# Pair-by-pair products in a PSUM tile of their own kind, halved first roots, and a newly searched order

## The chip, the cores and the metric

The kernel runs on one core of a Trainium2 chip. The metric is the device time of one launch in microseconds. A core has five instruction streams: TensorE (matmul, with its weight loads shown apart), VectorE, ScalarE, GpSimd, and SyncE, which only issues DMAs here. Matmul results land in PSUM, of which a core has eight banks.

## What is computed

Three blocks in a row, on 4 batches of 448 tokens and 768 features (12 heads of 64): attention with RMS-normalised queries and keys, a spatial gating block (called MoE in the program), and a mixer over tokens and channels.

```python
q_n, k_n = rmsnorm(q, g_q), rmsnorm(k, g_k)
scores = q_n @ k_n.T / sqrt(64)
attn = exp(scores - max) / (sum + 1e-09)
x = attn @ v                                   # heads side by side: (4, 448, 768)

h = relu(x @ w_in); u, v = h[..., :512], h[..., 512:]
v_n = (v - mean(v)) / sqrt(var(v) + 1e-06)
gated = u * (w_spatial @ v_n + b_spatial)
x = gated @ w_out

u = x + w_tok2.T @ relu(w_tok1.T @ x)          # over tokens
out = u + relu(u @ w_ch1) @ w_ch2
```

All inputs are float32. Most products are taken with operands split into a high and a low part and three matmuls (high by high, high by low, low by high: PASSES in the program).

## The kernel before

The heads are worked in pairs, 24 in all, six to a batch. For a pair the kernel squares and sums Q and K, takes the reciprocal roots, rescales, transposes Q and K on TensorE (`transposed`), multiplies scores in four row groups of 112 tokens (`scores`, c from 0 to 3, two heads each), takes the maximum on VectorE and the exponential on ScalarE, transposes the exponentials (`turned`), multiplies them with V (`values`), and leaves the pair's output as a high and a low part in a tile xp. The first eight pairs use plain float32 matmuls (WHOLE), the others the split. `slot(s)` lists the pieces of one step, which work on pairs s - 1 to s + 2.

The very first pair has a path of its own, `first` (line 794): K's squares on ScalarE (`squares`), their sum on VectorE and the roots on VectorE (`root`, through `rsqrt`, line 698), the rescaling of K on VectorE (`scale`), its transposes, and the copy out of PSUM on ScalarE, scaled by gg, the product of the two gains, which `start` (line 1009) computes on VectorE. Q of the first pair isn't rescaled: its roots, worked out on GpSimd, go into the exponential as its scale.

The MoE of a batch (`moe`, line 1218) starts with four groups of 128 tokens (the last of 64, padded by its low parts), each a PSUM tile vps. A group is the sum over the six pairs of the batch, with three matmuls of 512 columns for each pair, 18 in all: `xs[j]`, the xp tile of pair j, by `wv[:, w, j]`, the split weights of that pair's features. `prepare_v` makes wv beside the attention, on ScalarE, VectorE and GpSimd. The helper `run` issues the 18 in three pieces of six.

Nothing runs in the order in which it is written. Every call is kept as an operation in a `Plan`, and `issue` (line 413) puts them in order: `place` (line 272) simulates the engines with estimated costs and takes, of the operations that are ready, the one with the smallest weight; the weights come from rounds forwards and backwards, and are then changed by the numbers in NUDGES, each of which moves the weights of some operations about one place by a drawn amount (`nudged`, line 516). NUDGED bounds where that place may lie. The plan knows that VectorE and GpSimd share a port (`op.port`, line 176) and that a change between half-array and full-array matmuls costs TensorE time.

PSUM's eight banks are given out by `Banks` (line 132) in kinds: sc for scores, tp for transposes, mm for everything else before the mixer, values and vps among them. OWN says how many banks are kept for a kind; here two for sc, two for tp and one for mm, so three are spare. Tiles of a kind are opened in the order in which the program lists them, so a vps listed after a values tile can't be opened before it. BACK says how far back in its kind a tile's predecessor is taken to be in the backward round. Every instruction shows line 464, that of the call in `issue`; tiles tell them apart.

Of the kernel before, what the change touches and what calls it, by code (L numbers as in the profile page):

```python
# [15 lines left out]
AF = mybir.ActivationFunctionType  # L16
ALU = mybir.AluOpType
# [114 lines left out]
class Banks:  # L132
# [3 lines left out]
    OWN = {"sc": 2, "tp": 2, "mm": 1}  # L136
# [16 lines left out]
class Plan:  # L153
# [8 lines left out]
    def add(self, engine, fn, args, kwargs):  # L162
# [6 lines left out]
        if out is None:  # L169
# [7 lines left out]
            len(sbuf) > 1 and free(sbuf[1].shape) > 1  # L177
            or len(ins) == len(sbuf) and fn in ("tensor_scalar", "tensor_copy"))
# [288 lines left out]
BACK = {"sc": 4, "tp": 2, "mm": 2}  # L467
# [4 lines left out]
NUDGED = 4000  # L472
NUDGES = (
# [21 lines left out]
)  # L495
ENGINES = "gpsimd", "scalar", "sync", "tensor", "vector"
IDLE, SPARE, PACE = 1500, 200, 546
SHARED = {"vector": "gpsimd", "gpsimd": "vector"}


# [61 lines left out]
def attention_moe_mixer(  # L562
# [14 lines left out]
    P = 128  # L577
# [1099 lines left out]
```

## Time and profile before

| | us |
|---|---|
| median of 3 runs | 847.92 |
| fastest and slowest of them | 847.16, 848.81 |
| the profiled execution | 847.23 |
| span of its instructions | 845.2 |
| TensorE busy | 833.1 |
| VectorE busy | 674.7 |
| ScalarE busy | 526.7 |
| GpSimd busy | 344.6 |

The span runs from the first to the last instruction; the profiled execution took 2.0 us more than it. Busy times are sums over stages of different character: up to about 120 us the first batch's attention runs with preparation of weights beside it, up to 406 us attention and MoE are mixed, and after that TensorE works on the last MoE and the mixer. The granted TensorE clock is full throughout. In the rows below, a name like vps<-wv,xp gives the tile that is written and the tiles that are read, and x12 the number of instructions that a line merges.

### The profile page before, as it was taken

What the parts mean: (1) busy time and instruction counts of PE and PEld (TensorE: products, weight loads), DVE (VectorE), ACT (ScalarE), POOL (GpSimd) and SP (SyncE); (2) the same over time, 40 slices, a digit from 0 to 9 for tenths busy, and PEclk for the clock granted to TensorE, in tenths of its full rate; (3) what the DMA queues carried; (4) which work ended last, traced back from release to release, by engine and by line L of the source; (5) the groups of instructions that cost most, each with busy time, mean ns of one, the idle gap of its engine ahead of it and who ended that gap; (6) DMA issues with size and microseconds to landing.
All of it is one profiled execution on the core that took longest, in us unless ns stands there. A gap on an engine that the chain in (4) does not pass through costs nothing.

```text
span 845.2 us, 16488 instructions
## 1 busy us (share of the span) xinstructions
PE 833.1 (99%) x5530; PEld 700.4 (83%) x5530; DVE 674.7 (80%) x1340; ACT 526.7 (62%) x1268; POOL 344.6 (41%) x431
## 2 busy tenths in 40 slices
PE   7999999999999999999999999999999999999998
PEld 5454567777678876787799999999999999999998
DVE  6899899886787778787475677988889876998863
ACT  6999899897776878766343565554345654343331
POOL 2457555663445524242152222525331018515460
PEclk9999999999999999999999999999999999999999
DMA  6656676766765866466968787667555635742441
GB/s 170 161 160 185 177 232 184 236 169 170 241 184 144 216 171 196 124 180 194 331 201 247 234 275 252 220 197 221 156 175 175 214 123 161 226 140 84 140 142 66
DMA packets 158532, 157.94 MB, mean 187 GB/s; under 512 B 79216, under 2 KB 141616, under 8 KB 158448
## 3 DMA queue, kind: packets, MB, share of 16 engines
q1 hardware_dynamic: 157984, 156.86, 62.1%
q8 instruction: 44, 0.72, 0.4%
q14 instruction: 40, 0.33, 0.1%
q10 hardware_dynamic: 464, 0.03, 0.0%
HBM read 117.95 MB, written 38.88 MB: 186 GB/s over the span
## 4 chain that ended last, share of the span: by engine, by line
PE 82%; ACT 9%; DMA 3%; DVE 3%; issue 1%; SPq 1%; POOL 0%; ACTq 0%; POOLq 0%; DVEq 0%
PE o_ps L464 18%; PE h2ps L464 18%; PE xps L464 7%; PE ups L464 7%; PE av L464 6%; PE vps L464 5%; PE tp L464 5%; PE sc L464 4%; PE sps L464 4%; ACT e L464 4%; PE h1ps L464 4%; PE u_ps L464 3%; ACT et L464 2%; ACT sq L464 1%; DMA raw<-in_k_dram 1%
## 5 line engine op out<-in xcount | busy, mean ns | idle before, releaser
L464 PE MATMUL h2ps<-op,w 128*128 128x448 f32 x756 | 154.1, 366 | 0.0
L464 PEld LDWEIGHTS o_ps<-w,op 128*128 128x128 f32 x900 | 154.0, 188 | 0.0
L464 PE MATMUL o_ps<-w,op 128*128 128x384 f32 (+1 forms) x900 | 153.9, 332 | 0.0
L464 PEld LDWEIGHTS h2ps<-op,w 128*128 128x128 f32 x756 | 141.6, 188 | 11.2
L464 ACT ACTIVATE e<-sc,nm 112x448 f32<-112x448 f32 x184 | 121.7, 692 | 5.5 <-DVE nm L464 5.3
L464 DVE TENSOR_REDUCE nm<-sc 112x1 f32<-112x448 f32 x192 | 110.2, 615 | 8.0 <-PE sc L464 7.3
L464 ACT ACTIVATE op<-c 128x768 fp32r<-128x768 f32 x49 | 41.5, 847 | 83.7 <-PE o_ps L464 77.3
L464 POOL TENSOR_TENSOR src<-src 128x384 f32<-128x384 f32 x48 | 61.2, 1284 | 73.4 <-DMA src<-c_d 56.1
L464 PEld LDWEIGHTS tp<-ident,e 64*128 64x128 f32 (+2 forms) x1120 | 55.5, 139 | 27.4 <-ACT e L464 9.5
L464 ACT ACTIVATE et<-tp 128x448 f32<-128x448 f32 (+1 forms) x144 | 72.7, 560 | 4.9 <-PE tp L464 4.5
L464 DVE TENSOR_SCALAR word<-word 128x256 f32<-128x256 f32 (+5 forms) x132 | 60.5, 462 | 18.4 <-ACT word L464 17.3
L464 DVE SCALAR_TENSOR_TENSOR word<-raw,word 128x256 uint32<-128x256 uint32 (+2 forms) x132 | 71.2, 541 | 1.8
L464 POOL TENSOR_TENSOR u<-u,o 128x384 f32<-128x384 f32 x28 | 40.5, 1464 | 68.4 <-ACT o L464 38.9
L464 PE MATMUL tp<-ident,e 48*128 48x48 f32 (+2 forms) x1120 | 65.4, 232 | 1.2 <-ACT e L464 0.8
L464 PE MATMUL ups<-xp,wu 128*128 128x448 f32 x288 | 65.9, 368 | 0.0
L464 DVE TENSOR_TENSOR op<-c,op 128x768 fp32r<-128x768 f32 x49 | 54.6, 1115 | 10.3 <-ACT op L464 10.3
L464 PE MATMUL av<-et,v 128*64 128x448 f32 x288 | 61.1, 550 | 1.4 <-ACT e L464 0.9
L464 PEld LDWEIGHTS ups<-xp,wu 128*128 128x128 f32 x288 | 53.7, 188 | 6.4 <-ACT e L464 0.7
L464 DVE TENSOR_TENSOR c<-c,h2ps 128x448 f32<-128x448 f32 x84 | 49.7, 613 | 8.4 <-PE h2ps L464 8.2
L464 PE MATMUL xps<-wo,g 128*128 128x384 f32 x288 | 55.1, 340 | 0.0
L464 PE MATMUL sc<-kt,qt 64*112 64x448 f32 x384 | 52.9, 384 | 0.0
L464 PE MATMUL vps<-wv,xp 128*128 128x512 f32 x216 | 52.8, 397 | 0.0
(146 smaller groups left out, 1595.1 us busy)
## 6 DMA issues: line engine op xcount, KB each, us to landing
src<-c_d SPq DMA_DIRECT2D x132, 192.0 KB
wu<-wu_d SPq DMA_DIRECT2D x16, 768.0 KB
wo<-wo_d SPq DMA_DIRECT2D x16, 768.0 KB
raw<-in_moe_w_ch_dram SPq DMA_DIRECT2D x36, 256.0 KB
raw<-in_moe_w_ch_dram SPq DMA_DIRECT2D x24, 384.0 KB
raw<-in_q_dram SPq DMA_DIRECT2D x48, 112.0 KB
over<-over_d SPq DMA_DIRECT2D x48, 112.0 KB
u<-u_d SPq DMA_DIRECT2D x28, 192.0 KB
```

What stands on the lines that cost most here:

```text
L464: getattr(getattr(self.nc, op.engine), fn)(*args, **kwargs)
```

## The change

The edits, with the two lists of NUDGES cut. 233 numbers take the place of 231.

```diff
-    OWN = {"sc": 2, "tp": 2, "mm": 1}
+    OWN = {"sc": 2, "tp": 2, "mm": 1, "av": 0}
...
         op.port = engine == "gpsimd" and bool(sbuf) or engine == "vector" and (
-            len(sbuf) > 1 and free(sbuf[1].shape) > 1
-            or len(ins) == len(sbuf) and fn in ("tensor_scalar", "tensor_copy"))
+            len(sbuf) > 1 and (fn == "tensor_tensor" or free(sbuf[1].shape) > 1)
+            or len(ins) == len(sbuf) and fn in ("tensor_scalar", "tensor_copy") and free(ins[0].shape) > 1)
...
-BACK = {"sc": 4, "tp": 2, "mm": 2}
+BACK = {"sc": 4, "tp": 2, "mm": 2, "av": 1}
...
-NUDGED = 4000
+NUDGED = 4006
 NUDGES = (
...
-    for i in range(max(0, at - reach), min(len(weight), at + reach)):
+    for i in range(max(0, at - reach), min(NUDGED, at + reach)):
...
                 if on is nc.scalar:
-                    on.activation(sq, raw[:, a], AF.Square)
+                    for h in (slice(0, C), slice(C, n)):
+                        on.activation(sq[:, h], raw[:, a, h], AF.Square)
...
-                nc.vector.reduce_sum(ss[:T], sq, axis=AX.X)
+                for h in (slice(0, C), slice(C, n)):
+                    nc.vector.reduce_sum(ss[:T, h], sq[:, h], axis=AX.X)
...
-            for a in range(2) if i else (1,):
+            if not i:
+                roots = self.r[0][1][:T]
+                for c in range(0, C, 2):
+                    raw = self.raw[0][:, 1, c:c + 2].rearrange("p c r d -> p (c r) d")
+                    nc.vector.tensor_tensor(
+                        raw, raw, roots[:, 2 * c:2 * c + 4].unsqueeze(2).to_broadcast([T, 4, D]), op=ALU.mult)
+                return
+            for a in range(2):
...
-            nc.scalar.activation(t, tpf, AF.Copy, scale=1.0 if a == 0 else self.gg[:, 0:1])
+            if a and not i:
+                n = S // 2
+                nc.scalar.activation(t[:, :n], tpf[:, :n], AF.Copy, scale=self.gg[:, 0:1])
+                nc.vector.tensor_scalar(t[:, n:], tpf[:, n:], self.gg[:, 0:1], None, ALU.mult)
+            else:
+                nc.scalar.activation(t, tpf, AF.Copy, scale=1.0 if a == 0 else self.gg[:, 0:1])
...
-            nc.vector.tensor_tensor(self.gg, g[:, 0:1], g[:, 1:2], op=ALU.mult)
-            nc.vector.tensor_scalar(self.gg, self.gg, float(D) ** -0.5, None, ALU.mult)
+            nc.gpsimd.tensor_tensor(self.gg, g[:, 0:1], g[:, 1:2], op=ALU.mult)
+            nc.gpsimd.tensor_scalar(self.gg, self.gg, float(D) ** -0.5, None, ALU.mult)
...
             self.scores(s, 0)
+            self.scores(s, 1)
             yield
             self.turned(s - 1, 2)
+            self.turned(s - 1, 3)
             yield
-            self.turned(s - 1, 3)
             self.transposed(s + 1, 0)
+            self.transposed(s + 1, 1)
             yield
-            self.scores(s, 1)
-            self.transposed(s + 1, 1)
             self.values(s - 1)
             yield
             self.scores(s, 2)
+            self.scores(s, 3)
             yield
...
-            self.scores(s, 3)
             self.divisors(s)
...
-            ps = mm_tile("vps")
+            ps = psum.tile([P, 512], "av" if b < 1 and t < 1 * P else "mm", "vps")
             vr = mp.tile([P, DU], F32, tag="vr", bufs=2, name="vr")
             if m == P:
-                yield from run(
-                    ps[:, :DU], [(xs[j][:, a, t:t + m], wv[:, w, j]) for j in range(KD) for a, w in PASSES], 6)
+                ops = [(xs[j][:, a, t:t + m], wv[:, w, j]) for j in range(KD) for a, w in PASSES]
+                if b == 0 and t == 0:
+                    for k in range(0, len(ops), 3):
+                        with nc.joined_up():
+                            for i, (lhs, rhs) in enumerate(ops[k:k + 3], k):
+                                nc.tensor.matmul(ps[:, :DU], lhs, rhs, start=not i, stop=i == len(ops) - 1)
+                        yield
+                else:
+                    yield from run(ps[:, :DU], ops, 6)
```

The first token group of the first batch gets a PSUM kind of its own, av, with no bank kept for it; its three matmuls of each pair are joined into one operation. The first pair's squares, sums and rescaling are made in halves, and the copy of its transposed K is shared by ScalarE and VectorE. The two operations of gg go to GpSimd. The pieces of a slot are listed in another order. The plan's rule on the shared port counts other operations. NUDGES is another list, and no longer reaches past operation 4006.

## Rows read from the trace of the kernel before

**Rows 1.** The page: TensorE's busy time, and its busy tenths in 40 slices.

```profile
PE 833.1 (99%) x5530; PEld 700.4 (83%) x5530; DVE 674.7 (80%) x1340; ACT 526.7 (62%) x1268; POOL 344.6 (41%) x431
PE   7999999999999999999999999999999999999998
```

**Rows 2.** Windows of 20 us: busy us of each engine, clock, DMA share, GB/s.

```profile
0.00:20.00 20.00, 14.80 (x91) 11.43 (x91) 11.75 (x31) 12.63 (x32) 5.72 (x23) 1.00 0.68 166
20.00:40.00 20.00, 19.07 (x114) 10.34 (x115) 17.02 (x39) 20.00 (x59) 9.83 (x17) 1.00 0.63 165
40.00:60.00 20.00, 19.12 (x117) 9.67 (x116) 18.08 (x42) 20.00 (x56) 10.11 (x17) 1.00 0.60 161
60.00:80.00 20.00, 19.70 (x120) 10.53 (x118) 19.79 (x46) 20.00 (x62) 14.05 (x19) 1.00 0.60 163
80.00:100.00 20.00, 18.87 (x124) 10.67 (x124) 16.91 (x45) 17.20 (x50) 12.72 (x22) 1.00 0.68 199
100.00:120.00 20.00, 19.38 (x109) 12.53 (x106) 18.46 (x54) 17.24 (x50) 9.78 (x16) 1.00 0.77 221
```

**Rows 3.** Timeline of the start: start us, us, engine, operation, idle before it.

```profile
5.32 0.63 ACT L464 ACTIVATE e<-raw 112x512 f32<-112x512 f32 x1 [3.31 <-DMA raw<-in_q_dram]
5.99 0.69 DVE L464 TENSOR_REDUCE ss<-e 112x8 f32<-112x512 f32 x1 [5.99 <-ACT e L464]
7.06 0.16 DVE L464 TENSOR_TENSOR gg<-g 128x1 f32<-128x1 f32 x1 [0.38 <-DMA g<-in_g_k_dram]
7.13 0.17 DVE L464 TENSOR_SCALAR r1a<-ss 112x8 f32<-112x8 f32 x1
...
8.62 0.69 DVE L464 TENSOR_TENSOR raw<-raw,r1y 112x512 f32<-112x512 f32 x1
...
10.01 0.63 ACT L464 ACTIVATE whole<-tp,gg 128x448 f32<-128x448 f32 x1 [1.28 <-PE tp L464]
...
10.70 3.26 PE L464 MATMUL sc<-whole 64*112 64x448 f32 x16 [0.72 <-ACT whole L464]
...
12.88 0.72 ACT L464 ACTIVATE e<-sc,nm,r0y 112x448 f32<-112x448 f32 x1
...
13.89 2.13 PE L456 MATMUL warm<-ident 128*128 128x128 f32 x8
```

**Rows 4.** VectorE's groups by shape up to 60 us: busy us, mean ns, idle.

```profile
L464 DVE SCALAR_TENSOR_TENSOR word<-raw,word 128x512 uint32<-128x512 uint32 x8 | 5.5, 684 | 0.0
...
L464 DVE SCALAR_TENSOR_TENSOR wpart<-raw,wpart 128x256 uint32<-128x256 uint32 x4 | 1.6, 410 | 0.0
```

**Rows 5.** GpSimd on wv, and on xp up to 130 us: ns, first and last start.

```profile
L464 POOL TENSOR_TENSOR wv<-word,wv x6: 1269/1274/1285, 31.5 to 78.6; 128x512 fp32r<-128x512 f32 x6
L464 POOL TENSOR_TENSOR xp<-over,xp x7: 1132/1138/1379, 60.4 to 120.1; 128x448 fp32r<-128x448 f32 x7
```

**Rows 6.** TensorE's timeline from 80 to 110 us.

```profile
94.68 1.39 PE L464 MATMUL vps<-wv,xp 128*128 128x512 f32 x5
95.90 0.45 PE L464 MATMUL tp<-ident,e 112*128 112x112 f32 x3
96.12 1.85 PE L464 MATMUL vps<-wv,xp 128*128 128x512 f32 x7
...
101.34 2.48 PE L464 MATMUL av<-et,v 128*64 128x448 f32 x12 [0.53 <-DVE over L464]
103.74 3.02 PE L464 MATMUL vps<-wv,xp 128*128 128x512 f32 x12
```

**Rows 7.** TensorE's timeline from 28 to 60 us: bursts of scores.

```profile
32.92 1.01 PE L464 MATMUL sc<-whole 64*112 64x448 f32 x4
...
34.68 2.58 PE L464 MATMUL sc<-whole 64*112 64x448 f32 x8
...
49.23 1.76 PE L464 MATMUL sc<-whole 64*112 64x448 f32 x8
```

**Rows 8.** The chain of waits from 70 to 125 us: start us, us, what.

```profile
96.91 3.66 DMA over<-over_d
```

42 rows, old and new, of the table NUDGES are left out of this document.

## The prediction

> **What bounds the kernel now.** I read the page first, for the busy shares; then a table of 20 us windows, to see which engine fills each stage; then the timeline of the start and TensorE's own timeline up to 110 us, stretch by stretch, for what a burst costs and where it waits. The page says that TensorE is busy 99% of the span and that its slices are full from the second to the last but one [rows 1]. A busy matmul may also be a waiting one, so this alone does not tell what an edit is worth. The windows do. From 120 us to the end nothing shows but TensorE at 20.00 of 20 (the page's slices), so that part is a fixed amount of TensorE work and can only become shorter if some of it is done earlier. From 20 to 80 us ScalarE is at 20.00 of 20 and TensorE at 19.07 to 19.70; from 80 to 120 us neither is full [rows 2]. So the gain to be had is TensorE time that is idle before 120 us: 5.20 us in the first window and 0.93 + 0.88 + 0.30 + 1.13 + 0.62 = 3.86 us in the other five [rows 2], 9.1 us of 845.2 together. Every edit is worth what it takes out of those.
>
> **The first pair's roots.** The chain is: square K on ScalarE at 5.32, sum on VectorE at 5.99, ready at 6.68; then r1a at 7.13, and the rescaling of K at 8.62, the copy of its transposes at 10.01, the first exponential at 12.88 [rows 3]. Between 6.68 and 7.13 VectorE stands at gg, which waits 0.38 us for its DMA and takes the place ahead of r1a [rows 3]. Moving gg and its scaling to GpSimd takes out this wait: about 0.40 us (0.45 less an ordinary step of some 0.05). On GpSimd's queue the two ops wait for the same DMA; behind them comes the first work on r0 after 10 us, so this costs nothing as long as the square of Q on GpSimd is not put behind them (if it is, it is late by at most about 2 us, and r0's chain has that cover only in part). gg is needed at 10.01, three microseconds later.
>
> Halves of 256 in place of 512: the nearest rows that show a VectorE operation at both widths give 410 and 684 ns [rows 4], so a half costs 0.6 of a whole. Square plus sum was 0.63 + 0.69. In halves the first square is done 0.38 after 5.32 and its sum 0.41 later; the second sum starts behind the first and ends at about 5.32 + 0.38 + 0.82 + two steps of 0.04 = 6.60, against 6.68. That is 0.08; I take 0.05. The rescaling in halves ends at 8.62 + 0.82 rather than 8.62 + 0.69, while two of the four transposes start 0.28 earlier: out of it comes 0 with ends of minus 0.15 and plus 0.15. The kt copy split between ScalarE and VectorE turns 0.63 into about 0.4: 0.2, if VectorE is free at that time, and minus 0.3 if its half stands behind a 0.68 sum. I take 0.1. Sum of the start: **0.5 us**, ends 0 and 0.85. It reaches the span because ScalarE is full from about 10 us on [rows 2]: what ScalarE starts earlier, it ends earlier. If r0's chain on GpSimd holds the first exponential instead, this cover is gone and the 0.5 falls to 0.
>
> **The products pair by pair.** The first token group takes 18 products of 512 columns. In the trace they run as 5 and 7 at 94.68 and 96.12 and the last six at the head of the burst of twelve at 103.74 [rows 6]. Twelve show 3.02 us and five 1.39, so seven more cost 1.63, 0.233 each, and all 18 are 4.2 us of TensorE. After the change three products may go as soon as their pair and their slice of wv are there, in a bank that belongs to no ring of the others. The low parts of the pairs are written on GpSimd from 60.4 on, the last of wv at 78.6 [rows 5]; both may move earlier. So 12 to 15 of the 18, 2.8 to 3.5 us, can leave the stretch after 94 us where TensorE is nearly dense and go into idle time before it. How much idle is there? From 40 to 100 us 0.88 + 0.30 + 1.13 [rows 2], plus 0.53 before the value burst at 101.34 [rows 6], plus waits inside bursts: two score bursts of eight at 34.68 and 49.23 took 2.58 and 1.76 [rows 7], so 0.8 us of the first is waiting. That is 2.84 to 3.6 us. Against it stand three more beginnings of a burst. The five took 95.90 - 94.68 = 1.22 from their start to the next burst's, where 5 x 0.233 is 1.17, so a beginning next to full-width transposes costs 0.05; next to scores it costs more: a score burst of four shows 1.01 us and one of eight 1.76, so four more cost 0.75, and 0.26 of the 1.01 is beginning and tail [rows 6, 7]. I take 0.3 for the three. The gain lies between minus 0.5 and plus 2.8; I take **1.7**, some 60% of the idle filled, as the waits that rows 6 and 7 show are 0.5 and 0.8 us long and a group of three needs 0.7.
>
> What a switch costs decides how much of this is kept, and it differs by what stands beside it: 0.26 beside scores, 0.05 beside transposes, and transposes are what follows the five [rows 6, 7]. Rival D takes the dear price. The rule against this change stands in the Trainium skill, "TensorEngine Tiling (Array Packing)", section Key Properties: a change of tiling mode, not just of tile, drains TensorE. The rows agree with it beside scores; beside the transposes of 112 rows they show next to no drain.
>
> **The remaining edits.** The slot lists scores 0 and 1 together and 2 and 3 together, but within each kind of PSUM tile the order of the tiles stays as it was (scores 0 to 3; turned 2, 3, transposed 0, 1, turned 0, 1; one values). Only starting weights of the order change. The port rule of the planner counts small two-input VectorE operations and leaves out small one-input ones: no instruction is added. All of it, with the new numbers in NUDGES and the cut at 4006, is a newly drawn order of the first 4006 operations. No row prices that; I put it at 0 and bound it by the idle of rows 2: at best 3.86 and some 2 of the start's filler, at worst as much again, and I hold the middle, plus or minus 1.5, for likely.
>
> **Sum.** 0.5 + 1.7 + 0 = 2.2 us. The profiled execution took 847.23 (span 845.2 and 2.0 around it); it would come to 845.0. The median of the runs is 847.92, 0.7 above it, so the forecast is 845.7.
>
> **Rivals.** (A) The products stay where they were. The planner still ranks an operation by how late it may be; it lets the first xp wait until 60.4 us [rows 5], and it may let the groups wait until 94 us as well. Then the change does not do what it says, and only the start is left: 847.9 - 0.5 = 847.4. For it: ScalarE is full, so whatever is not urgent is put off. Against: TensorE takes what is ready when nothing else is.
>
> (B) The open bank holds up the scores, and it is slower. One of eight banks is held from the first group to the last, some 40 to 70 us, and sc, tp, mm and av then leave two spare instead of three. A score burst that must wait for the exponentials to free a bank shows its price already: 2.58 against 1.76 for the same eight matmuls [rows 7], 0.8 us. Six pairs have two such bursts each. With three more stalls the gain is gone, with five it is slower by over 0.2%; with seven it is 847.9 - 2.2 + 5.6 = 851.3. Against: the tile that was opened at 94.68 held a bank too, and two spare banks still give the scores four. The Trainium skill's "PSUM — Partial Sum Buffer", in Summary: rules for kernel authors, asks to evacuate promptly since PSUM is tight; a bank held this long goes against that, and no run so far shows what it costs.
>
> (C) The new order also removes the waits at the end of the stage. TensorE idles 0.53 before 101.34, behind a DMA of over that took 3.66 us from 96.91 [rows 6, 8], and the start runs a filler (warm) for 2.13 us from 13.89 [rows 3], in which transposes of the first exponentials could have gone. With 0.5 of the start, 2.8 of the products and 2 of these the time is 842.6.
>
> (D) The groups of three land between scores and values rather than between transposes. Then each of the six has a switch on either side, 6 x 2 x 0.26 = 3.1 us [rows 7], where three bursts at that price would be 1.6 today: 1.5 off instead of 0.3, 0.5 left of the 1.7, and 847.9 - 1.0 = 846.9. For it: half of TensorE's work in this stage is scores and values. Against: the planner counts a switch as a cost. What the Trainium skill says of a change of tiling mode ("TensorEngine Tiling (Array Packing)", Key Properties) is this drain, taken at its full price.
>
> **How the numbers follow.** Chances: the forecast 0.40, with its own range of 843.5 to 847.2; A 0.20; B 0.12; C 0.12; D 0.10; a new order that simply loses 1.5 to 4 us, 0.06. A measurement of this kernel tells about 0.2%, 1.7 us, from no change, so faster means below 846.2 and slower above 849.6. Of the forecast 0.33 lies below 846.2 and 0.07 above; with C that is 0.45 faster. A, D, the 0.07 and 0.02 of the last make 0.39 same; B and the rest of the last make 0.16 slower. The range leaves out half of C below and B with some of the last above: 842.5 to 850.0.
>
> **What would show it.** gg on GpSimd and r1a within 0.1 us of the sum's end shows the first step; a first score burst at 10.2 rather than 10.70 [rows 3] the start. Products of vps in threes before 90 us show the second step, and TensorE's idle of 20 to 120 us must fall from 3.86 to about 2; every stage after 110 us should begin some 2 us earlier. If vps first appears at 94 us, it is A. If score bursts of eight last 2.5 us more often than before, it is B. The prediction is wrong if the idle before 120 us is unchanged and the time is not, for then the order after 120 us matters, which I have put at nothing.

## The result and the profile after

The changed kernel is slower: a median of 852.38 us (four runs, 851.74 to 853.53) against 847.9 for the kernel before in the same runs, a ratio of 1.0051 with a 95% interval of 1.0038 to 1.0064. That is 4.5 us more, where 2.2 less was forecast. The profiled execution took 851.89, span 850.1, 4.9 more than the span of before.

The page of the changed kernel gives TensorE's busy time:

```profile
PE 833.9 (98%) x5522; PEld 701.3 (82%) x5522; DVE 667.9 (79%) x1342; ACT 526.0 (62%) x1269; POOL 353.9 (42%) x433
```

TensorE is idle for 850.1 - 833.9 = 16.2 us of the span, and was for 845.2 - 833.1 = 12.1 us before [rows 1]. So 4.1 of the 4.9 us are idle time and 0.8 is longer busy time.

Where the time lies is seen in the windows first: each line is a stretch, its length, the busy us of TensorE, of its weight loads, of VectorE, ScalarE and GpSimd, and then the granted clock, the DMA share and GB/s.

```profile
0.00:20.00 20.00, 14.05 (x75) 10.07 (x76) 12.08 (x32) 11.05 (x28) 5.55 (x24) 0.91 0.72 169
20.00:40.00 20.00, 18.47 (x108) 9.23 (x107) 17.81 (x40) 20.00 (x58) 8.44 (x17) 1.00 0.52 141
40.00:60.00 20.00, 19.37 (x119) 10.05 (x117) 16.97 (x38) 19.81 (x57) 9.88 (x14) 1.00 0.59 153
60.00:80.00 20.00, 18.81 (x118) 10.17 (x117) 19.29 (x49) 19.64 (x59) 14.93 (x23) 1.00 0.53 155
80.00:100.00 20.00, 19.85 (x117) 11.83 (x117) 18.01 (x45) 18.60 (x53) 12.46 (x17) 1.00 0.67 183
100.00:120.00 20.00, 19.23 (x134) 10.75 (x130) 15.78 (x40) 16.43 (x48) 12.47 (x22) 1.00 0.63 181
120.00:140.00 20.00, 19.13 (x151) 14.45 (x153) 18.46 (x58) 16.87 (x48) 9.42 (x15) 1.00 0.74 220
140.00:160.00 20.00, 19.26 (x181) 13.81 (x178) 19.23 (x46) 16.81 (x48) 10.85 (x20) 1.00 0.68 206
```

TensorE's idle time from 20 to 120 us is 1.53 + 0.63 + 1.19 + 0.15 + 0.77 = 4.27 us, where before had 3.86 [rows 2]; and from 120 to 160 us, where before was full, 0.87 + 0.74 = 1.61 more. The first window has 0.75 more idle time (14.05 for 14.80 busy) and a clock of 0.91. Two stretches gained, 40 to 60 us (19.37 for 19.12) and 80 to 100 us (19.85 for 18.87), and the others up to 160 us lost. The remaining 1.3 us of idle time lies in single waits after 160 us.

The start, from the timeline (start, us, engine, operation, in brackets the idle time before it and what ended it), beside [rows 3]:

```profile
5.54 0.72 ACT L464 ACTIVATE e<-raw 112x256 f32<-112x256 f32 x2 [3.54 <-DMA raw<-in_q_dram]
6.30 0.75 DVE L464 TENSOR_REDUCE ss<-e 112x4 f32<-112x256 f32 x2 [6.30 <-ACT e L464]
7.08 0.17 DVE L464 TENSOR_SCALAR r1a<-ss 112x8 f32<-112x8 f32 x1
7.46 0.19 POOL L464 TENSOR_TENSOR gg<-g 128x1 f32<-128x1 f32 x1 [1.03 <-DMA g<-in_g_k_dram]
...
10.10 0.45 ACT L464 ACTIVATE whole<-tp,gg 128x224 f32<-128x224 f32 x1 [1.43 <-PE tp L464]
...
10.59 0.45 DVE L464 TENSOR_SCALAR whole<-tp,gg 128x224 f32<-128x224 f32 x1
...
11.09 4.96 PE L464 MATMUL sc<-whole 64*112 64x448 f32 x16 [1.09 <-DVE whole L464]
...
14.69 0.67 ACT L464 ACTIVATE word<-raw 128x512 f32<-128x512 f32 x1 [1.68 <-DMA raw<-in_moe_w_in_dram]
...
15.26 0.71 ACT L464 ACTIVATE e<-sc,nm,r0y 112x448 f32<-112x448 f32 x1
```

gg now waits on GpSimd (7.46) and r1a follows its sum at once, but the sums begin only when both squares are through (6.30 = 5.54 + 0.72 + 0.04), because the searched order takes the second half's sum first. The plan sees no loss in that, since in it both sums wait for the second square: behind a `rearrange`, `Part` no longer tells the halves apart. So r1a comes at 7.08, not 0.45 earlier than 7.13. The halves of the K copy run one behind the other, scores begin at 11.09 instead of 10.70, and the same sixteen matmuls take 4.96 us instead of 3.26. Then ScalarE stands 1.68 us for a load of w_in, which the new order has put ahead of the first exponential: 15.26 instead of 12.88. Of these 2.4 us the plan had 0.6 itself: it puts the first exponential at 12.8, and that of before at 12.2.

The products do what the change says. TensorE's timeline from 84 to 110 us, and ScalarE's at 116 us:

```profile
85.59 0.95 PE L464 MATMUL vps<-wv,xp 128*128 128x512 f32 x3
...
88.86 0.95 PE L464 MATMUL vps<-wv,xp 128*128 128x512 f32 x3
...
93.14 0.96 PE L464 MATMUL vps<-wv,xp 128*128 128x512 f32 x3
...
95.30 1.62 PE L464 MATMUL vps<-wv,xp 128*128 128x512 f32 x6
...
107.67 0.97 PE L464 MATMUL vps<-wv,xp 128*128 128x512 f32 x3
```

```profile
116.77 0.58 ACT L464 ACTIVATE sq<-raw 128x448 f32<-128x448 f32 x1 [2.17 <-DMA vrest<-in_v_dram]
```

Nine products are done by 94.1 us, where before had begun none [rows 6]. But at 116.77 ScalarE stands 2.17 us for a load of the next pairs.

One more measure is used from here on. The kernel's planner gives every instruction a start time of its own, and the trace has the true one. **Slip** is the second less the first, taken as the median over ScalarE's instructions that were planned in the 10 us (50 us from 300 on) that begin at the time at the head of the column, in the profiled execution of each kernel. The planner's whole span is 846.1 us for the kernel before and 845.9 for the changed one: it holds them for equal. The last three lines belong to experiments below.

```
planned at us        0     20     50     80    110    140    190    300    800
before            +0.8   +0.8   +1.1   +1.2   +0.6   +0.3   -0.8   -2.3   -3.3
changed           +0.8   +2.3   +3.0   +2.4   +4.7   +5.4   +3.7   +2.6   +1.8
order B           +0.5   +1.9   +2.5   +3.1   +7.1   +7.0   +8.9   +8.3   +6.8
order C           +0.8   +0.8   +1.1   +2.3   +4.1   +3.8   +5.3   +3.0   +1.4
robust old        +1.1   +1.1   +1.4   +1.6   +0.6   +0.8   +1.8   -0.2   -1.2
```

Against before the changed kernel is 1.5 us late at 20 us, 1.9 at 50, 4.1 at 110 and 5.1 at 140, and from there to the end the difference stays between 4.5 and 5.1. So against its own plan the changed kernel loses all of it before 140 us, in two stretches: the start, and that between 80 and 140 us.

### The profile page after: what moved, and what is told of

Read it like the earlier page. It is cut to its first block, busy times and chain, and to the rows that moved or that the text cites. A ratio compares the mean times of both kernels' runs of the same rounds, so it can differ in the third digit from the quotient of the medians.

```text
span 850.1 us, 16425 instructions
## 1 busy us (share of the span) xinstructions
PE 833.9 (98%) x5522; PEld 701.3 (82%) x5522; DVE 667.9 (79%) x1342; ACT 526.0 (62%) x1269; POOL 353.9 (42%) x433
## 4 chain that ended last, share of the span: by engine, by line
PE 82%; ACT 6%; DVE 4%; DMA 4%; SPq 2%; POOL 1%; issue 1%; POOLq 0%; ACTq 0%; DVEq 0%
PE o_ps L464 18%; PE h2ps L464 18%; PE xps L464 7%; PE tp L464 6%; PE av L464 6%; PE ups L464 6%; PE vps L464 5%; PE sc L464 5%; PE sps L464 4%; PE h1ps L464 4%; PE u_ps L464 3%; ACT e L464 3%; SPq L464 2%; DMA raw<-in_moe_w_ch_dram 1%; DVE wpart L464 1%
## 5 line engine op out<-in xcount | busy, mean ns | idle before, releaser
L464 ACT ACTIVATE e<-sc,nm 112x448 f32<-112x448 f32 x184 | 118.3, 664 | 3.9 <-DVE nm L464 3.5
L464 POOL TENSOR_TENSOR src<-src 128x384 f32<-128x384 f32 x48 | 63.6, 1334 | 74.6 <-DMA src<-c_d 58.7
L464 DVE TENSOR_SCALAR word<-word 128x256 f32<-128x256 f32 (+5 forms) x132 | 55.3, 425 | 21.9 <-ACT word L464 21.0
L464 ACT ACTIVATE et<-tp 128x448 f32<-128x448 f32 (+1 forms) x144 | 68.4, 533 | 5.0 <-PE tp L464 4.7
```

What stands on the lines that cost most here:

```text
L464: getattr(getattr(self.nc, op.engine), fn)(*args, **kwargs)
```

## The experiments

In all of them the kernel's own planner runs first. Where an edit moves an operation, the planned order is frozen, one operation is taken out and put in at another place of it, and all else keeps its order ("ahead" or "behind" an operation by its number). The function that does this is the same in all and is left out of the edits shown. In the texts on record, theory L is that the two waits for loads (word at 14.69, sq at 116.77) are the loss, theory P that the early products are.

### One place at a time, in the changed kernel

**e1**: the w_in copy behind the fourth exponential.

```diff
+MOVES = (("behind", 249, 108),)
```

> The changed kernel, its order kept as it is, with one operation moved on ScalarE: the first step on the second slice of w_in (word, at 14.69 us), which waits 1.68 us for its load, goes behind the first pair's fourth exponential. Theory L (the new order puts operations on ScalarE ahead of the landing of their loads, and the order after them carries the delay to the end): 852.4 falls by 1.4 to 2.0, to about 850.7. Theory P (the products pair by pair cost it: the held bank, the switches): unchanged, 852.4. Theory C (the lower TensorE clock in the first score burst costs it): at most 0.5 less, as the maxima still come late.

Measured 851.22 (848.95 to 855.55), ratio 1.0047 [1.0028, 1.0066]. The first exponential came at 12.76, 2.5 us earlier, but the median fell by only 1.2, with an interval that overlaps the changed kernel's, and the runs spread over 6.6 us. A new wait stands at 16.12: 1.13 us for the load of the next Q.

**e3**: pair 10's squares behind the next exponentials.

```diff
+MOVES = (("behind", 1258, 1193), ("behind", 1260, 1162))
```

> The changed kernel, its order kept, with the two squares of K of pair 10 moved on ScalarE: the first of them waits 2.17 us at 116.77 for a load; it goes behind the copy of the transposed Q of pair 9, some 3 us later in the order, the second one operation group later, and the sum between them goes with them. Theory L: 852.4 falls by 1.5 to 2.3, to about 850.4. Theory P and theory C: unchanged, 852.4.

Measured 853.14, ratio 1.007 [1.0057, 1.0084]: nothing is gained. The wait of 2.17 is gone, and in its place an exponential waits 1.04 us at 116.78 and a w_out copy 1.06 at 121.87.

**e4**: both moves, and eight filler matmuls on TensorE ahead of K's transposes and the first scores, so that the clock holds.

```diff
+MOVES = (("behind", 249, 108), ("behind", 1258, 1193), ("behind", 1260, 1162))
+FILL = {57: [7] * 5, 95: [7] * 3}
```

> The changed kernel with both moves, and with eight filler matmuls on TensorE (five ahead of the first pair's K transposes, three ahead of its first scores), so that the granted clock may stay up in the first score burst. Theory L with C as a small part: 3.5 to 4.5 less than 852.4, about 848.4, and the clock of the first 20 us back at 1.00. Theory P: at most 0.5 less.

Measured 851.6, ratio 1.0052 [1.004, 1.0064]. The clock stayed at 1.00 and the first burst took 3.27 us, but the filler put the scores off to 12.74. The burst so ended at 16.01, as in the changed kernel (11.09 + 4.96 = 16.05), and the first exponential came at 14.78. e4 trades the lower clock for a later start and can't price it. Whole executions can: of those with a mean granted clock of 1.000 over the span, one of order C (below) took 854.06 and one of robust 3 853.19, where the eight of the kernel before beside e4 took 846.53 to 848.37. A lower clock is therefore not needed for a loss of this size. It can be a share of it: the four runs of the changed kernel have a mean of 0.997, those of before 0.999, and 0.002 of 850 us is 1.7 us (an estimate, and an upper bound, as it takes every cycle lost for time lost).

**e7**: the early groups of products back behind 100 us.

```diff
+MOVES = (("ahead", 1040, 1115), ("ahead", 1055, 1115), ("ahead", 1064, 1115),
+         ("ahead", 1075, 1115), ("ahead", 1105, 1115))
```

> The changed kernel, its order kept, but the first five of the six groups of three products go behind each other to the place just ahead of the sixth, at about 107 us, where all of the first token group's products then stand in one burst. Theory P: what the groups cost by switches between 85 and 97 us is saved, 0.5 to 1.5 less than 852.4. Theory L: the groups are the gain that the other waits hide; moving 15 products of 0.233 us back into a stretch where TensorE is nearly dense costs 1 to 3 us, 853.4 to 855.4.

Measured 853.08, ratio 1.0062 [1.0049, 1.0075], 0.7 above the changed kernel with overlapping intervals. Theory P, which wanted 0.5 to 1.5 less, falls: early products show no loss in this order, and may be a small gain. Of theory L's waits, e1, e3 and e4 show no gain clear of the noise; the largest is e1's 1.2 of 4.5.

### The edits without the order, and other orders

**e9**: the kernel before with its order frozen, and only the start edits put into it, where an operation is issued (first half ahead of second).

```diff
+    if i in (11, 12):                 # gg
+        return [("gpsimd", fn, args, kw)]
+    if i == 37:                       # K's squares
+        return [("scalar", fn, (args[0][:, x], args[1][:, x], args[2]), kw) for x in h]
+    if i in (39, 59):                 # both sums
+        return [("vector", fn, (args[0][:, x], args[1][:, x]), kw) for x in h]
...
```

> The kernel before with its written order frozen, and the start edits alone put into it: gg on GpSimd, pair 0's squares of K on ScalarE and both sums in two halves (first half first), the rescaling in two, the K copy half on ScalarE and half on VectorE, the VectorE half ahead of the sum of pair 1. No product moves and no order is searched. Theory S (the start edits cost the time: their extra fixed costs, later first scores and the fall of the clock behind them) expects 849 to 852 against 847.7 before. Theory O (the loss is in the newly searched order, not in the instructions) expects 847.2 to 848.2. My forecast of these edits was a gain of 0.5, 847.2.

Measured 847.91 (11 runs) against 847.6, ratio 1.0004 [0.9995, 1.0012]. Its timeline of the start:

```profile
5.44 0.73 ACT L463 ACTIVATE e<-raw 112x256 f32<-112x256 f32 x2 [3.45 <-DMA raw<-in_q_dram]
...
5.90 0.74 DVE L463 TENSOR_REDUCE ss<-e 112x4 f32<-112x256 f32 x2 [5.90 <-ACT e L463]
...
6.68 0.17 DVE L463 TENSOR_SCALAR r1a<-ss 112x8 f32<-112x8 f32 x1
...
9.52 0.42 DVE L463 TENSOR_SCALAR whole<-tp,gg 128x192 f32<-128x192 f32 x1
...
9.97 0.47 ACT L463 ACTIVATE whole<-tp,gg 128x256 f32<-128x256 f32 x1 [1.29 <-DVE whole L463]
...
10.50 3.27 PE L463 MATMUL sc<-whole 64*112 64x448 f32 x16 [1.09 <-ACT whole L463]
...
11.83 0.61 DVE L463 TENSOR_REDUCE nm<-sc 112x1 f32<-112x448 f32 x1
...
12.23 0.20 POOL L463 TENSOR_TENSOR r0y<-r0y,r0z 112x8 f32<-112x8 f32 x1
...
12.59 0.19 POOL L463 TENSOR_TENSOR nm<-nm,r0y 112x1 f32<-112x1 f32 x1 [0.16 <-DVE ra L463]
...
12.81 0.72 ACT L463 ACTIVATE e<-sc,nm,r0y 112x448 f32<-112x448 f32 x1
```

Here the halves do overlap: the first sum starts at 5.90, before the second square is through. r1a comes at 6.68 (7.13 before), scores at 10.50 (10.70), and the first exponential at 12.81 (12.88 [rows 3]). The gain of 0.45 at r1a is 0.20 at the scores and 0.07 at the exponential, and nothing at the end. The exponential waits for VectorE's maximum (ready at 12.44) and GpSimd's root of Q (r0y ready at 12.43), not for the scores. So the start edits cost nothing and bring nothing that can be measured, and the 4.5 us are not theirs.

**Orders A and B** are the changed kernel with other numbers in NUDGES, searched from other seeds for the smallest planned span; **order C** is the kernel before with a new search of the same kind.

```diff
-NUDGES = (10000021, 10000032, ...)
+NUDGES = (50000013, 50000027, ...)
```

> The changed kernel's instructions, all of its edits kept, with another order that I searched for it in the same way from other seeds; the planner's own span is 844.0 (845.9 for the order that was shipped, 846.1 for the kernel before). Theory O expects a time that differs from the changed kernel's 852.4 by more than 1.5 us (anywhere from 845 to 850, or from 854 on), since orders that the planner holds equal are not equal on the chip. Theory E (the edits of instructions cost the time, whatever the order) expects 850.5 to 853, less the 1.9 that the planner gives at most.

> As order A, from other seeds again; the planner's span is 845.3, within 0.6 of the shipped order's. Theory O expects a time unlike the shipped order's 852.4 by more than 1.5 us and unlike order A's by something other than the planner's 1.3. Theory E expects 851 to 853.

> The kernel before, none of the change's edits, with another order searched in the same way; the planner's span is 846.8, 0.7 over that of the order it shipped with. Theory O expects that this moves the time by more than 1 us from the planner's 848.4, either way, most likely up (849.5 to 853), since the shipped order of before would then be the lucky one. Theory E expects 848 to 849.

The column "over plan" is the median less the planner's span; the runs named "robust" come next. Each ratio is taken against the runs of before beside it, whose medians were 847.90 for the changed kernel, 847.60 for A to C, and 847.88 for the robust orders.

| instructions | order | planner's span | median us | ratio [95%] | over plan |
|---|---|---|---|---|---|
| before | its own | 846.08 | 847.60 | 1 | 1.5 |
| changed | its own | 845.91 | 852.38 | 1.0051 [1.0038, 1.0064] | 6.5 |
| changed | A | 844.04 | 850.37 | 1.0031 [1.0020, 1.0042] | 6.3 |
| changed | B | 845.33 | 856.55 | 1.0107 [1.0092, 1.0123] | 11.2 |
| before | C | 846.78 | 854.06 | 1.0073 [1.0061, 1.0085] | 7.3 |
| changed | robust 1 | 845.72 | 854.56 | 1.0076 [1.0059, 1.0094] | 8.8 |
| changed | robust 2 | 845.20 | 854.86 | 1.0079 [1.0063, 1.0096] | 9.7 |
| changed | robust 3 | 845.33 | 851.53 | 1.0040 [1.0026, 1.0054] | 6.2 |
| before | robust old | 845.98 | 850.03 | 1.0024 [1.0013, 1.0034] | 4.1 |

Order A fits both theories; B and C fit theory O alone. Order C shows that a new order is enough: not one instruction of the change is in it, and it is 6.5 us slower than the same instructions in their old order, although the planner sees 0.7. What is not shown by a run is all of the change's edits in the frozen old order; only the start (e9) and nine of the products (e10) were put there. All redrawn orders lie 4.1 to 11.2 us over their plan, the changed kernel's 6.5 in the midst of them. It is the old order that stands apart, with 1.5.

What a bad order looks like is plainest in order B, the slowest. Windows of 3 us, and TensorE's timeline:

```profile
90.00:93.00 3.00, 1.48 (x12) 1.01 (x9) 2.97 (x7) 0.17 (x1) 2.32 (x4) 1.00 0.31 71
93.00:96.00 3.00, 2.29 (x7) 0.80 (x7) 2.84 (x8) 3.00 (x9) 0.00 (x0) 0.86 0.18 39
96.00:99.00 3.00, 3.00 (x15) 2.47 (x15) 2.71 (x7) 3.00 (x12) 0.72 (x1) 0.57 0.71 186
```

```profile
93.61 0.41 PE L464 MATMUL tp<-ident,e 112*128 112x112 f32 x2 [2.13 <-ACT e L464]
...
94.22 1.98 PE L464 MATMUL sc<-whole 64*112 64x448 f32 x4
```

At 90 us ScalarE runs dry (0.17 of 3.00 busy) behind VectorE's maxima, TensorE behind ScalarE for 2.13 us, and then the granted clock falls to 0.57, near its lower level of 1.2 GHz: four score matmuls take 1.98 us where [rows 7] has 1.01. One wait is so paid twice. Order A and robust 1 show the same pair, an idle of 1.18 and of 1.88 us and then 0.58. In the kernel before, TensorE has no wait above 0.9 us between 18 and 200 us, and five over 0.3, 3.0 us in all; in order B there are ten over 0.3, 6.7 us in all, in the changed kernel eleven, 6.0.

**Robust orders.** Does the planner err in something that can be put into it?

```diff
-NUDGES = (10000021, 10000032, ...)
+NUDGES = (70000000, 70000006, ...)
```

> All edits of the change, in an order searched anew for another aim. Theory R: the planner's orders come out 1.5 to 11 us over its span because each engine then keeps its order while (a) the port that the planner shares between VectorE and GpSimd goes to whoever comes first, and (b) loads land later than planned. So each order was played through again with the planner's own costs, the order of every engine fixed, the port first come first served, and landings 0, 0.3 and 0.6 us late; the mean delay against the plan over the first 440 us is 5.2 us for the kernel before, 6.9 for the changed one, 10.2, 8.1 and 6.4 for orders A, B and C. The search took plan plus that delay as its aim: here plan 845.7, delay 0.7. R expects 845 to 848 (6 below the changed kernel, as the delay is). Theory E (the edits themselves cost 4 us) expects 851 to 853. Plain luck of the draw, not bound to the port or the landings, expects 849 to 857 as orders A to C gave.

> As the first robust order, from other seeds: plan 845.2, delay 0.9. R expects 845 to 848 again; plain luck 849 to 857; theory E 851 to 853.

> The same aim, but begun from the shipped order of the changed kernel and not from none: plan 845.3, delay 1.4 (from 6.9). R expects 845.5 to 848.5; plain luck 849 to 857; theory E 851 to 853.

> The kernel before, none of the edits, the same aim begun from its own shipped order: plan 846.0, delay 2.9 (from 5.2). R expects a gain of up to 2.3, so 845.3 to 847.6; plain luck 847 to 853, since the shipped order is then the best of several draws and any other is worse.

All four lie above what theory R expected, the three of the changed kernel by 3.0 to 6.9 us over the top of it and the old one by 2.4; the two with the smallest worked-out delay are among the slowest. Of the first five kernels the one with the smallest delay (before, 5.2) is also the least over its plan (1.5), but order A has the largest (10.2) and is only 6.3 over. R falls: an order searched for a small delay is not fast for that. Robust old, the neighbour of the old order, has the lowest median of the eight redrawn ones, and is still 2.2 us slower than the order that it started from.

### What stayed open

**e10**: the products taken forward in the kernel before.

```diff
+MOVES = (("behind", 1021, 971), ("behind", 1022, 1021), ("behind", 1023, 1022),
+         ("behind", 1024, 913), ...
+         ("behind", 1050, 914), ...)
```

> The kernel before in its own frozen order, no other edit: nine of the eighteen products of the first token group are taken forward, three behind the scores at 91.7 us, three behind the value bursts at 92.65 and three behind those at 93.45, in the bank that the tile has anyway (free from 90.7). My sum's term (12 to 15 products moved into idle time, 1.7 us) would make this at least 1.0 faster, 846.6. Against it: TensorE is already full from 88 to 100 us in the kernel before, so the products only push the transposes back; this expects 847.4 to 848.5.

Measured 848.68 (11 runs) against 847.4, ratio 1.0013 [1.0004, 1.0021]: 1.1 us slower by the ratio (0.3 to 1.8), where the term of the sum wanted 1.0 or more faster. Windows of the kernel before and TensorE's timeline of this one:

```profile
84.00:88.00 4.00, 3.60 (x23) 1.55 (x20) 3.77 (x12) 3.37 (x10) 3.11 (x5) 1.00 0.86 241
88.00:92.00 4.00, 4.00 (x26) 2.11 (x26) 3.60 (x10) 3.88 (x13) 1.44 (x5) 1.00 0.42 124
92.00:96.00 4.00, 4.00 (x22) 1.94 (x19) 3.50 (x9) 3.25 (x12) 2.60 (x4) 1.00 0.62 178
96.00:100.00 4.00, 4.00 (x38) 3.09 (x38) 2.65 (x8) 2.71 (x7) 2.24 (x3) 1.00 0.64 203
```

```profile
92.91 0.97 PE L466 MATMUL vps<-wv,xp 128*128 128x512 f32 x3
93.81 0.97 PE L466 MATMUL av<-et,v 128*64 128x448 f32 x4
94.71 0.96 PE L466 MATMUL vps<-wv,xp 128*128 128x512 f32 x3
95.60 0.97 PE L466 MATMUL av<-et,vrest 128*64 128x448 f32 x4
96.50 0.96 PE L466 MATMUL vps<-wv,xp 128*128 128x512 f32 x3
97.30 0.83 PE L466 MATMUL tp<-ident,e 112*128 112x112 f32 x7
...
111.07 1.17 PE L466 MATMUL vps<-wv,xp 128*128 128x512 f32 x4
```

From 88 us on there is no idle time to fill. A group between value bursts takes 0.90 us from its start to the next burst's, where its three products are 0.70: a switch costs about 0.2 there, and 0.1 beside transposes (96.50 to 97.30). The four products at 111.07 stand in the timeline of the kernel before like this:

```profile
110.66 1.17 PE L464 MATMUL vps<-wv,xp 128*128 128x512 f32 x4
```

They are 0.41 us later in e10, but a score burst ahead of all moved products is 0.22 later already (85.64 for 85.42). So in these two executions the moved products cost 0.2 us net; the spans differ by 0.8 (846.0 for 845.2).

**e12**: the changed kernel's start put right. **e13**: that, and e3's moves.

```diff
+MOVES = (("ahead", 40, 41), ("ahead", 49, 50), ("ahead", 63, 64),
+         ("behind", 73, 62), ("behind", 249, 108))
```

> The changed kernel in its own frozen order with the start put right: first halves ahead of second halves (sums, rescaling), VectorE's half of the K copy ahead of the sum of pair 1, and the load wait of the w_in slice behind the fourth exponential. First scores at 10.5 (from 11.09), first exponential at 12.8 (from 15.26), as with the same edits in the old order. If the loss is in places (2.0 of the 4.5 lie in the first 20 us): 850.4. If a cure comes back as other waits: 851.4 to 852.5.

> As the one before, and the two squares of pair 10 that wait for their load at 113 to 117 us moved behind the next exponentials. If the loss is in places: 2.0 and 1.9 come back, 848.5. If spread: 851 to 852.5.

Measured 852.44 (ratio 1.0057 [1.0042, 1.0072]) and 853.73 (1.0075 [1.0059, 1.0092]): no gain from either. In e12 scores begin at 10.47 as expected and the first exponential at 13.55 (12.8 was expected), 1.7 earlier than in the changed kernel, but by 20 us only 0.5 of it is left in the slip (1.8 for 2.3), and waits of 1.6 us (an exponential, between 60 and 80 us) and 1.8 (sq at 116 us) follow. e13 has the same order as e12 up to 110 us and in its profiled execution only 0.4 of that first wait. In its place it shows order B's pair further on:

```profile
121.87 0.86 PE L466 MATMUL sc<-kt,qt 64*112 64x448 f32 x5 [0.94 <-ACT e L466]
```

```profile
120.00:123.00 3.00, 2.06 (x21) 1.22 (x23) 2.05 (x8) 2.19 (x8) 0.13 (x1) 0.98 0.68 217
123.00:126.00 3.00, 3.00 (x20) 1.62 (x17) 3.00 (x9) 2.60 (x7) 1.73 (x3) 0.50 0.65 175
```

So none of the cures tried (e1, e3, e4, e12, e13) brought back more than 1.2 us, and in the traces a cure at one place came back as a wait at another. That the loss belongs to the order as a whole fits this; a place that nobody tried is not ruled out.

**e8**: the changed kernel's load wait put into the old order.

```diff
+MOVES = (("ahead", 239, 96),)
```

> The kernel before in its own frozen order with one operation moved: ScalarE's copy of the second w_in slice stands ahead of the first exponential, as in the changed kernel, and waits there for its load. The first exponential should come 1 to 2 us later than 12.88. If time lost at the start comes through to the end (ScalarE is full from 20 to 80 us): 848.7 to 849.7. If it is made up before the end: 847.4 to 848.2.

Measured 849.46 against 847.4, ratio 1.002 [1.001, 1.003], so 1.7 to 2.1 us. ScalarE's timeline and the windows:

```profile
14.13 0.66 ACT L466 ACTIVATE word<-raw 128x512 f32<-128x512 f32 x1 [1.32 <-DMA raw<-in_moe_w_in_dram]
14.69 0.71 ACT L466 ACTIVATE e<-sc,nm,r0y 112x448 f32<-112x448 f32 x1
```

```profile
15.00:18.00 3.00, 2.28 (x8) 1.40 (x8) 2.37 (x9) 3.00 (x10) 0.38 (x2) 0.82 0.32 70
18.00:21.00 3.00, 2.35 (x14) 2.35 (x14) 2.73 (x6) 3.00 (x9) 0.87 (x2) 0.50 0.83 255
```

The first exponential is 1.8 us late, and the end 1.7 to 2.1 (0.8 to 2.5 by the interval): in the old order, where ScalarE is full up to 80 us [rows 2], lost time at the start comes through to the end. The profiled execution has the lower clock from 18 to 21 us as well, but two executions with a mean of 0.999 and 1.000 took 849.05 and 849.89, so the loss does not hang on it. One operation at a wrong place costs some 40% of what the whole change cost. In the changed kernel, taking the same wait out (e1) brought at most 1.2.

No version that beats both kernels came out of this: e9 equals the kernel before, all others are slower.

## Why the prediction was wrong

**The order, put at 0, is the step that failed.** The prediction saw that the new numbers in NUDGES make "a newly drawn order of the first 4006 operations", found no row that prices it, took the middle of the idle of rows 2 and held plus or minus 1.5 for likely, with 0.06 for an order that loses. The whole change measured +4.5. Less what its instructions cost in the old order (e9 nothing, e10 1.1), the order's share is 3.4 to 4.5, an estimate that takes the parts to add up. Seven other draws, five of them with the edits, cost between +2.2 and +9.0, each against the runs of before beside it; not one of them is below 0. The middle was the wrong value, since the old order is no middle: it ends 1.5 us over its plan where the redrawn ones end 4.1 to 11.2 over theirs. A row could have hinted at it: [rows 2] shows TensorE waiting 3.9 us in 100 and the clock at 1.00 in every window, and an order has far more ways to be worse than that than better. Whether the old order was picked by its time on the chip or came so by luck, the runs can't tell.

**The start, 0.5, measured nothing in the old order (e9, 0.3 slower with an interval that holds 0).** The first sub-step was right where it can be seen: r1a 0.45 earlier in e9, as 0.40 and 0.05 had been put down. The K copy was mis-sized: I took it as parallel halves, 0.63 to 0.4, and it is 0.42 and 0.47 in a row, 0.9 in all. The second half starts 0.03 to 0.04 us after the first has ended, in both kernels, whichever engine goes first. The Trainium skill's "PSUM — Partial Sum Buffer", section PSUM bank collisions raise a hardware error, states a rule that asks for this: two engines are not to access the same PSUM bank in the same partition at once. The rows of both kernels agree with it. The changed kernel's plan has it built in: in `add`, a read of a PSUM tile depends on every earlier read of it by another engine. And the case that the prediction named, "if r0's chain on GpSimd holds the first exponential instead, ... the 0.5 falls to 0", is what e9 shows, with VectorE's maximum ready at the same time. It should have been the forecast: in [rows 3] the first exponential already comes 2.18 us behind the first scores, and the chain between them had not been read. In the changed kernel the new order made a loss of the start, 2.4 us at the first exponential.

**The products, 1.7, measured -1.1 in the old order (e10, nine products at places from 92.9 us on), and 0.7 with overlapping intervals in the new one (e7).** The term was mis-sized. The idle time was counted over windows most of which the products cannot use: 40 to 80 us, before enough of xp is there, and 80 to 88, where the tile in its old kind gets a bank only at 90.7 (the change, with a kind of its own, put one group of three there, at 85.59). Windows of 4 us would have shown that in the old order TensorE is full from 88 us on, where the rest could go. The price of a switch, 0.05 to 0.26, was sound: 0.1 beside transposes and 0.2 beside values. The Trainium skill's rule that a change of tiling mode drains TensorE ("TensorEngine Tiling (Array Packing)", Key Properties) agrees with the 0.2, between 128x128 products and 128x64 values; products and transposes of 112 rows both count as full-array in the plan, so the rule asks nothing of the 0.1. The trace of e10 places 0.2 us of the 1.1 where the products were moved; where the rest goes was not found.

**The rivals.** A fell, with products at 85.59. B shows in no row: the changed kernel's bursts of eight scores from 84 to 110 us took 2.09, 1.76 and 1.71, one of them above the 1.76 of [rows 7], the products that hold the bank take 23 us from first to last (85.59 to 108.64) and not 40 to 70, and products put back late (e7) did not help. D's price was about right, but its time, 846.9, was not. C took the new order for a gain. The sentence on what would make it wrong came nearest: idle before 120 us did not fall (4.27 for 3.86), and of the idle time that came in, 0.41 us lies from 20 to 120 us and 1.61 from 120 to 160 us, in the order "which I have put at nothing".

## What to carry to other kernels

A change that makes a planner search its order anew is two changes, and the second can be the larger: freeze the old order, put the edits into it, and measure that first. An order that suits the chip can be worth more than the edits, and a new one of nearly the same planned span is a draw: here all eight, the change's own among them, lost 2 to 9 us. Idle time counts as room for moved work only in windows as short as the work, in which its inputs and its bank are there.

## What the runs showed of the hardware that was not expected

A wait of TensorE costs more than its length where the granted clock falls after it. After idle times of 1.18, 1.88 and 2.13 us (order A, robust 1, order B) the granted clock was 0.57 or 0.58 in a window of 3 us, and a burst of four scores took 1.68 us in A and 1.98 in B instead of 1.01; the first burst of the changed kernel, at 0.50 from 12 to 15 us, took 4.96 instead of 3.26. It does not fall alike in every execution: e10 starts as the kernel before does, and shows 0.59 from 18 to 21 us where that has 1.00. In e13 the total goes with the clock: the three executions with a mean granted clock of 0.994 took 854.64 to 855.61, and the three with 0.996 to 0.998 took 852.27 to 852.82. In order B it does not (854.85 at 0.996, 858.92 at 0.998). The clock is not all of the loss, as order C and robust 3 took 854.06 and 853.19 at a mean of 1.000.
